# Two more landing places for the first weights, and a new order for every operation of a one-core attention and feed-forward kernel

## The chip, the cores and the metric

The kernel runs on one core of a Trainium2 chip. The core has a matrix engine (TensorE, PE in the profile), a vector engine (VectorE, DVE), a scalar engine (ScalarE, ACT), a general engine (GpSimd, POOL) and a queue engine (SyncE, SP) that here issues every DMA transfer. Each engine works through its own instructions in the order in which the program gives them, and waits on semaphores for the others. The metric is device time in microseconds.

## What is computed

Attention over four batches of eight heads with 768 positions of 64 values each: every position sees its neighbours nearer than 16 positions and, beside them, one maximum of the keys and one mean of the values for each of 24 blocks of 32 positions. Its output, 4 x 768 rows of 512, goes through a normalization and a feed-forward layer with a residual:

```python
scores_l = scale * np.matmul(q, k.transpose(0, 1, 3, 2))        # where |i - j| < 16
scores_s = scale * np.einsum('bhsd,bhnd->bhsn', q, k_sum) + np.log(block)
a = softmax(np.concatenate([scores_l_m, scores_s], axis=-1))
x = a @ np.concatenate([v, v_sum], axis=2)                      # heads side by side: 512
xn = (x - mu) / np.sqrt(var + 1e-06) * g_ln
out = x + np.maximum(xn @ w_ch1, 0.0) @ w_ch2                   # 512 -> 2048 -> 512
```

The two weights reach the kernel as eight bytes an element, so each is 8 MB in 16 tiles of 512 KB.

## The kernel before

**Tiles and stages.** The rows are cut into 24 tiles T of 128, taken in pairs g (12 pairs) by the feed-forward layer. The first batch's six tiles are done early, in 12 halves t, in float32 and straight from the inputs: `early_k` copies the window of the keys into a cleared buffer (POOL and ACT), `early_qk` multiplies (PE), `softmax` (DVE, then ACT), `early_transp` and `early_pv` (PE). The other three batches go through `heads` in split float16. `ln` normalizes a tile, `lnT` transposes it by DMA. `g1(s)` makes a 256-wide part of the middle values h of one pair (24 matrix instructions of 256 columns), `g2(s)` adds its part to the output (12 more, of 512 columns; "a" in the profile). 96 such parts make the feed-forward layer.

**Weights.** For each tile f of w1, `fetch_w(f, 1)` brings 512 KB into a buffer with the tag `raw`, of which there are four (RAW = 4), taken in turn; `merge_w` (one TENSOR_SCALAR and two SCALAR_TENSOR_TENSOR on DVE) makes 32-bit values m of it, after which the buffer is free; `gram` and, for each quarter of w1, `scale_w1` find a scale; `split_w` makes the two float16 halves that `g1` multiplies by. The same is done for w2, whose one scale (`scale_w2`) needs all 16 tiles. No `g2` can start before that.

**Middle values.** The values h lie in 14 buffers, taken in turn, each for two steps s: `y0` and `y1` first (YB = 2), then twelve buffers `x0` to `x11` that hold keys, queries and values of the early attention before.

**The order.** The program first records 2808 operations (an operation is one instruction, or a few of PE that stay together) with what each depends on. Then `Plan.issue` chooses the order in which they are given to the engines: `schedule` is a list scheduler with assumed durations and waits, which lets each engine take, of the operations that are ready, the one with the lowest rank. Before, the rank was worked out from the longest path to the end plus one stored number for each step (`ORDER`), improved in three rounds of a schedule forward and a schedule backward (`ROUNDS`), and then shifted by one stored number for each step and engine (`SHIFT`); a last schedule gave the order. Nothing of it exists on the chip but that order: an instruction there starts when its engine comes to it and what it depends on is done.

Of the kernel before, what the change touches and what calls it, by code (L numbers as in the profile page):

```python
# [19 lines left out]
U32 = mybir.dt.uint32  # L20
# [6 lines left out]
P = 128  # L27
# [16 lines left out]
ROUNDS = 3  # L44
# [17 lines left out]
    "rD2DqDep@g{w+NjZZ>8QypmT2yyg*W*&Alv&PatHNeiDt3tOdH_Kiay1!Yp{CvZ*8yC8neHYtX8Q@}Bf8dChtZr*`&;@_dh>3<+LnwafqmOH@g"
    "L*9>yF<TO1=0wi*Xe=5|mY|~*5$t`^Yzw*=4fn+tSbI%sJuhdGSqzvY<x3INzVJ&a5v+YS!G))p%R1^oS6=8RA3hz)X-"
    "gBe@0M=B#SHY3g)U+~mo}lNkXup^Jbg?2fz-DKOuT=RuA&!*KcW@%8}PE(X0%fCgjxJXwD?;y=V#Duq**jN%YpwGwAX&M^cFpmPwbliN=v=X8b"
    "_P82gAX{^8({yu&IEr&Ob<RyokQ3FN>O1p|$N`eC;)}$9TVFzFEJnW{E@DKiKS<$I+}2e}P%p5Om|q9^xMZ!w}ZIfOZD7V*$0i&EMJe(sttYU1"
    "(NAkF_J;Pr*JBF5}3h?^*EpOnTPKYyyAxp+--"
    "%JDiwZs3CEJ*|KPKMID#G^)UKv2{hXuW;Pd0+<Sn@N@?a4vu_C7LOu!9dlG%TOJ2_r@5S+Ej`T`AdmHeN0q7(j?4scDI(_gH`aVO?A1Ia@&}$h"
    "QcR~BLW6kbgrB~2W&)=bCxClYJS?*?Oc+w<#-3JWLqQ779fxnacIzRfCc-`ST0{*KirB<IQ{*ivhcf!!zB`|-"
    "VXEfTrL4WxYs{~z)B$u)1=aE)i(be2X%`(vJ&v?!e>aEMBhxi^qzKxye|0pn~XWZfPYy<r9bVCQe<d%evX5a}<DR?6K@`8`jUS_e>9t_ql=w~O"
    "mJ&m6GliPzjsRQ^HvS)--8>YSSnkW~ul2(mv$3M_W5ghKu>&C*z=9y-TIj{Mm6b^R<=*|HwLdpG=-"  # L70
    "<u7Fi>Q8R6kg`h%l>F{7MMG6hAVyOk6uQDMJ_peqLuHSH=EV!+w|e%=;k6Z9wpWh-uGnRsz1Ro-qqCIY#JWF9&Kc@zi9=&OTTt+q-"
    "W^KfIp+NJbdxGv>KoHK|dS7`=wZB31^;0kMDu&LF#etZ*~RT%Zc;)A@U=Bf4prnG5&(DucWRQ*3kF#XCZ#(LLYDa1%Do9=1m``5GMhj-"
    "3wkhY0?+?Rwr;shO0&E;V?^@jYrQ!I}vc#fjn2SCVani3;!#?!|KrFc)o{n)<iTjFPGlHD_c0v6J8t0Gn8K4$R2OJsTXSlnMa@Cp_6wJ3s3bW#"
    "sPkd-<59Tg`umYCy4Eh52c`yJmUV9brs~ioxGfRABRRxv)+?^+jtkxFPu8MvNoNc2j6n>zb5idWUU*#=6x^S2cHq-"
    "Sb%Ql^V|vMo$!UdpQ2TG^8?3HX43H4W`5Kf!|y8k9z|d7p=aKqPuz;g58Ri6XAy>y8DzGN`Es8)<#_T@`tBxrPJpL7_?QQ}d<dp-oD;;^325de"
    "&T_!F3(-PX@-9N_3z!vE<P}M+6Tl&XXYE|GNa|^a2YwB9{W#Z;^-"
    "<)WON}0!yAfU8#BV;wUpMm%;`=#%=lQ+Kx{mnqJC~%xtc{>2Iug5ro@t=(yMbjY{ho_XGFP_gG4%h>`h9KB<9)enaK@L+Mt`*Khj-PX>q@k;8("
    "-M*74wGL50cMP@GK?YE@*Q(-yNr${Q&pwub90$6@O-bGhQ8ncE-`i>FD|)Ga?eb1TX`7fK_Y1MS@e0SLrG6F2U2wUZ-"
    "!E@4vuDGB|nSiAEeZJiiv4nkV5&XxXEM`stZ-@RG{?D;B=jl4BYDca44vWY&eil{?=T!c7`nw)X3Ba&Tl8rsH2ie?x-X=I<uFY9c-"
    "F!~G|cdOjf5d1`$CE_HbBKJZ)1-RCLvA?_$k=P)nUwQ2btYuA3kOa{+#=3)uwI?@9bVEH|s)Xe{<&@I;vJBiLu@V*I-"  # L80
    "FHmbTGoUWi%!_&}iG2gy+`f_C&Tiu*6})aUhc4suG4y*fx;18mE1De2y>K4f72pBO$)g=-bU<j+z-&D+@8M-"
    "N#EPRgqPYhRV@=w|HqRP|e%BML3eT-1u{r3j1g{&32ffCfg3)7n_(#@%z=&G2$?Xhxfh6jzC%?<|{(N-"
    "5pFEwJ0lmoMBD__TTQ#^G9l_nK^&W>VmXrIkLChlJ_CcRl@Z=xiyP6s1OMhKpE;=y73pwWmnpi!~Y&x~oaDFAcIN^_>c&i^Xw-"
    "Jug$)^R4xiYUam@k?1*CFO@5_i>DJbeKAIE*I*qN{pz(=ncYqqbvsSUSAaFbf{iZ%goCSMU!b?+M^hPF*$l*iblH%)MqZ|L<XsC-"
    "ZU_XZ{Z!wza_"
)
SHIFT = (
    "c-n<q34B%6(SO-NLV_TRtP(&Pftm`aZ3=z}h@?tE5<w!Os9;1=MA?LovI%aVh*1{V6cA9$5*9(x3W8CQAZ;ytAR?6=0z%j!$?Jde{+BoJzPWk%"
    "{Vw;ubLY%{X6DSf_<X^?(qH}liGII-R+-"
    "=LtKcvFMELuMFWGbE8@P(jhmSpKz|A$rc3%x2J5w4ycAvq^dSmQ0fB4*)QQ>gi4PJgS=8iPR#u#&J8E}&g{$>DfNsQ0eAJ4Iz)8<^@o@?l$hC%"  # L90
    "D;3*loQoeLdHG3Mo;4j)@lDV)c3m&4&YT?rq{y*_;IABqBSA651Cx3`r&cE$R92jc_J&&S&ESr`5O_AZ}z9sW63>0uE0D=Q9;#Q@*49z3Ka!3S"
    ";(Jm2a8Qw@A&oeib?d1arkYE1BVY~{fHUyAoM@OGQACSJw(ku!dOwg<frjWu`BfSYqN2-"
    "hgl=Nm;iUcb)9I}^IwToj6XHpbc{2Y>hG`(nlSKIo{qM;yq9-"
    "!!cic;0)}hWS10T;TGh4Cu5hDfoK;=awqEIaTcS9tB%$2EM;|#Ixcv;o}b(>$0ArHRp)m|8$MObIA!CZx!GucCD{lF!rF*cOK<@_h=BVE7m|Vb"
    "g<u8ukGPCqbWz_DBEsR5x-BlWIc+t5Tk6_hP)>!|I2}0YUBQ^3vVW_ZCEE0J?!<GF?PVv-x~GY8~pu)_<lTT<1L8x`8Gv|j{Smp$%>CLq|-"
# [24 lines left out]
    "PWkXE`XQ6s@_w1@7ka%d;M;>9*hm$_l#G1N@T9RD!oy}tln4;8@WCP!TAc|S4D`w&Kk_Y{WkjA+sw^Vix6|5(-"  # L120
    "Gj|w5oyjGoCft7aV(;a{r*@ch2J`sQy$e*YslLZ)2HHo2yvs^k6PHJmb2a{C!E=&c%AH#I;aFU33MnbLa<$3HKLVEh%R&zLWE@34C@~-"
    "UgUP#FtYR+^^0iUqguF2<$Ww^fqB)G47+m*Q18rk6`>$&goBD2s!>Dj#VRn9|C_N>8&pd#=2<wW()At(j$h|r++M0esYP=eHGjyjNL1-"
    "*(1)sNdAU{r$xBtL9R^ddm-L!z#TvRFA@F^(&yrHH_EdQ0LLlQI_BCFu-^hlf6kdCY`fK|NocoJzzkx|kVW5p3-"
    "s<FzAmtJ9}gXT;P9mUKgBr@arGX5=L_A3>AxQ2GY@p758n?yI^3!Gq?X3KAECbj2TuHic7KMnuZn%C|DJgF3yhHqWBysuxnivSrkFDcSCq2j%~"
    "rofVl{Y3QvSBus{b(d46bzwuF!y!zI8f)-"
    "%@L@vB96Lt4zq)Th&Z`4Scfy!gk$1P~q!h$nhL#bc7tS3Qkh?A{A#=yL?seJw{31b@isM1KnM&+VBhbWM%SsfO5^g6x^#hXQk4I>&Url`K|!=z"
    "CvF)gm<5K^sc%S|NE*wI6%KnQ1Xe55i<Q<5^evxi?H`&9kdjGN6vR@$lYQi@U<Cyv?d?2&exN_81gQCy*7NmfpYu=8J%xprV`&sjJ?J=rwN~md"
    "n{%6n7l}zHG}-hcL(2l<o~~O{71F6ZgYC9N(bU^C*|zf<C~Nkw1<2LAbD^R;0Dmn@;%9<_`sRb1Y-"
# [37 lines left out]
class Plan:  # L166
# [174 lines left out]
    def schedule(self, rank, after, back):  # L341
# [16 lines left out]
        for _ in range(count):  # L358
# [27 lines left out]
            if e == "sync" and not back:  # L386
                t = max(t, flight[0])
# [855 lines left out]
```

## Time and profile before

| | us |
|---|---|
| time, median of 3 runs | 616.39 |
| lowest and highest | 614.54 and 616.79 |
| profiled execution | 614.86 |
| its span, first to last instruction | 613.0 |
| around the span | 1.9 |

A busy share on the page is that of the span. The 40 digits of a row on the page are slices of 15.3 us. A bracket at the end of a timeline row gives the idle time of the engine just before the instruction and what ended it. Every operation is recorded by one helper, so all rows show its line, L425, and are told apart by the names of the tiles. Ends of matrix instructions are modelled: neighbours overlap in the rows, and what one costs in a dense stream is the distance between starts.

### The profile page before, as it was taken

The numbers are of one execution on the slowest core, as the hardware profiler recorded it, in microseconds if no ns is written. First come the engines' busy times: TensorE is split into PE (matmuls) and PEld (weight loads), VectorE is DVE, ScalarE is ACT, GpSimd is POOL, SyncE is SP. The second block draws the span as 40 slices with busy tenths as digits, with TensorE's granted clock in tenths as the row PEclk, the third lists the DMA queues.
The fourth block names the chain that finished last, engine by engine and source line by source line (L and its number), as shares of the span: only waits on it lengthen the run. The fifth ranks groups of instructions, "written<-read, shape, count | busy, mean of one in ns | idle before, by whom it ended". The sixth has DMA issues, their size and how long they took to land.

```text
span 613.0 us, 14238 instructions
## 1 busy us (share of the span) xinstructions
PE 602.3 (98%) x5347; PEld 414.0 (68%) x5347; DVE 399.4 (65%) x1098; ACT 343.9 (56%) x914; POOL 151.9 (25%) x279
## 2 busy tenths in 40 slices
PE   6999999999999999999999999999999999999997
PEld 5557778885454685676767864666775676678756
DVE  5799999998568379767694487367486574412211
ACT  3689986578867458576864364366465644111100
POOL 7232312102324124321331033133142333100000
PEclk9999999999999999999999999999999999999999
DMA  8989897454677636867886045526466332300000
GB/s 302 281 251 329 236 298 234 115 145 127 178 208 197 167 100 167 214 138 197 200 176 171 14 127 136 130 77 178 120 154 162 89 94 53 62 10 1 17 18 35
DMA packets 116396, 90.56 MB, mean 148 GB/s; under 512 B 69613, under 2 KB 100717, under 8 KB 116326
## 3 DMA queue, kind: packets, MB, share of 16 engines
q1 hardware_dynamic: 116326, 89.65, 54.1%
q8 instruction: 42, 0.69, 0.5%
q14 instruction: 28, 0.23, 0.1%
HBM read 67.05 MB, written 6.29 MB: 120 GB/s over the span
## 4 chain that ended last, share of the span: by engine, by line
PE 76%; DVE 10%; DMA 6%; ACT 4%; issue 2%; SPq 1%; POOL 1%; ACTq 0%; POOLq 0%
PE h L425 33%; PE a L425 31%; PE s L425 3%; DVE m L425 2%; PE o L425 2%; DMA bst<-in_ks 2%; PE low L425 2%; DMA bst<-in_qa 2%; SPq L425 1%; PE warm L425 1%; DVE kmax L425 1%; DMA qs<-in_qt 1%; DMA bst<-in_vs 1%; DVE h_x L425 1%; ACT p L425 1%
## 5 line engine op out<-in xcount | busy, mean ns | idle before, releaser
L425 PE MATMUL h<-xt,w_u 128*128 128x256 f16 x2304 | 264.1, 273 | 0.0
L425 PEld LDWEIGHTS <-w_u 128*128 128x128 f16 x2304 | 224.1, 98 | 37.1 <-issue 0.9
L425 PE MATMUL a<-w,h_x 128*128 128x512 f16 (+1 forms) x960 | 211.5, 374 | 0.1
L425 PEld LDWEIGHTS <-h_x 128*128 128x128 f16 x1008 | 97.8, 98 | 98.7 <-issue 0.4
L425 ACT ACTIVATE h_x<-h 128x512 f16<-128x512 f32 x80 | 46.8, 591 | 96.7 <-PE h L425 96.4
L425 DVE SCALAR_TENSOR_TENSOR h_x<-h,h_x 128x512 f16<-128x512 f32 x80 | 54.5, 684 | 68.1 <-ACT h_x L425 68.0
L425 ACT ACTIVATE p<-p,mn,sv 128x120 f32<-128x120 f32 x144 | 68.2, 475 | 10.0 <-POOL mn L425 9.9
L425 POOL TENSOR_TENSOR p<-p,p 128x480 f16<-128x480 f32 x36 | 42.5, 1184 | 64.1 <-ACT p L425 59.8
L425 ACT ACTIVATE bst<-bst 128x384 f32<-128x384 f32 (+2 forms) x55 | 32.3, 588 | 33.0 <-DVE vsum L425 12.7
L425 POOL TENSOR_SCALAR mn<-mn,sv 128x4 f32<-128x4 f32 x36 | 17.7, 491 | 114.4 <-DVE mn L425 110.4
L425 PE MATMUL a<-w,h_y 128*128 128x512 f16 x192 | 43.9, 379 | 0.0
L425 DVE SCALAR_TENSOR_TENSOR m<-raw,m 128x512 uint32<-128x512 uint32 x64 | 42.9, 681 | 0.2
L425 DVE SCALAR_TENSOR_TENSOR kl<-ksg,sv,kh 128x640 f16<-128x640 f32 x36 | 33.3, 925 | 11.6 <-ACT kh L425 11.3
L425 DVE CUSTOM_DVE_ANT_0 p<-s,mask 128x120 f32<-128x120 f32 x144 | 33.2, 274 | 11.1 <-PE s L425 9.1
L425 POOL TENSOR_TENSOR x<-x,rc 128x256 f32<-128x256 f32 x36 | 25.2, 706 | 52.1 <-DVE x L425 50.0
L425 DVE SCALAR_TENSOR_TENSOR qhl<-qs,sv,qhl 64x512 f16<-64x512 f32 x36 | 28.1, 779 | 12.2 <-ACT qhl L425 11.3
L425 ACT ACTIVATE v<-vst,sv 128x512 f16<-128x512 f32 x36 | 24.4, 712 | 19.6 <-PE o L425 17.8
L425 DVE SCALAR_TENSOR_TENSOR x<-a,scales,x 128x512 f32<-128x512 f32 (+1 forms) x24 | 17.7, 736 | 26.7 <-PE a L425 26.6
L425 ACT ACTIVATE kh<-ksg,sv 128x640 f16<-128x640 f32 x36 | 29.5, 819 | 9.3 <-DMA ksg<-in_kt 6.9
L425 ACT ACTIVATE qhl<-qs,sv 128x512 f16<-128x512 f32 x36 | 25.7, 713 | 13.6 <-DMA qs<-in_qt 10.2
L425 PEld LDWEIGHTS <-h_y 128*128 128x128 f16 x192 | 18.6, 98 | 20.2
L425 DVE SCALAR_TENSOR_TENSOR v<-vst,sv,v 128x512 f16<-128x512 f32 x36 | 27.2, 772 | 2.0 <-ACT v L425 1.9
(118 smaller groups left out, 698.8 us busy)
## 6 DMA issues: line engine op xcount, KB each, us to landing
raw<-in_w SPq DMA_DIRECT2D x32, 512.0 KB
ksg<-in_kt SPq DMA_DIRECT2D x36, 368.0 KB
qs<-in_qt SPq DMA_DIRECT2D x72, 128.0 KB
out_x<-x SPq DMA_DIRECT2D x23, 256.0 KB
bst<-in_ks SPq DMA_DIRECT2D x20, 192.0 KB
bst<-in_qa SPq DMA_DIRECT2D x15, 256.0 KB
bst<-in_vs SPq DMA_DIRECT2D x20, 192.0 KB
vst<-in_va SPq DMA_DIRECT2D x36, 96.0 KB
```

The costliest lines, as they stand in the source:

```text
L425: getattr(getattr(nc, self.ops[i].engine), op)(*a, **k)
```

## The change

`fetch_w` puts the raw tiles f = 4 and f = 5 of w1 into the buffers `y0` and `y1`, which are as large, 4096 bytes in each partition; the first values h to use these buffers (those of s = 0 to 3) then also depend on `merge_w(4)` and `merge_w(5)`. The four `raw` buffers are left to the other 14 tiles of w1, and to w2 as before.

`ORDER` becomes a table of 2808 numbers, one for each operation, in the order in which they are recorded; `SHIFT` and the rounds are gone. Each number, times 16 ns, is a wanted time, and the rank is this wanted time. `schedule` holds every operation back until 600 ns (AHEAD) before its wanted time. No matrix instruction, vector instruction or transfer is added or removed.

```diff
-ROUNDS = 3
 ORDER = (
...
-SHIFT = (
...
-    FLIGHT = 8
+    FLIGHT, AHEAD = 8, 600
...
-    def schedule(self, rank, after, back):
+    def schedule(self, rank, after):
...
-                heapq.heappush(coming[self.ops[i].engine], (0.0 if back else 1000.0, i))
+                heapq.heappush(coming[self.ops[i].engine], (max(1000.0, rank[i] - self.AHEAD), i))
...
-                    heapq.heappush(coming[self.ops[j].engine], (ready[j], j))
+                    heapq.heappush(coming[self.ops[j].engine], (max(ready[j], rank[j] - self.AHEAD), j))
...
-        rank, best = [r + early[x.stage] for r, x in zip(rank, self.ops)], None
-        for _ in range(ROUNDS):
-            start, end = self.schedule(rank, after, False)
-            if best is None or max(end) < best[0]:
-                best = (max(end), start, end)
-            rank = [-x for x in self.schedule([-x for x in end], then, True)[1]]
-        rank = [r + shift[x.stage, self.ENGINES.index(x.engine)] for r, x in zip(best[1], self.ops)]
-        self.start, self.end = self.schedule(rank, after, False)
+        wanted = np.cumsum(np.frombuffer(zlib.decompress(base64.b85decode(ORDER)), "<i4"))
+        self.start, self.end = self.schedule(16.0 * wanted, [self.waits(x) for x in self.ops])
...
-        d = raw[f, i] = work("raw", f"raw{i}_{f}", [P, DM, 2], U32, RAW)
+        if i == 1 and f in (4, 5):
+            d = raw[f, i] = place(f"y{f - 4}", "raw", [P, DM, 2], U32)
+        else:
+            d = raw[f, i] = work("raw", f"raw{i}_{f}", [P, DM, 2], U32, RAW)
```

The new table can be unpacked and its numbers laid beside the operations of the kernel before. They are scattered, many are negative (first of all), and they are ranks rather than times of the chip. Those that the prediction speaks of:

```
operation (engine)                                   wanted, us
early_k(0), copies of the first key window (POOL)    -60.0 to -51.1
clear(): kx, second half (POOL)                       10.5
clear(): ends of the key rows (POOL)                  -41.0, -33.7, -26.0, -1.5, -0.2, 14.8, 14.8, 15.5
clear(): vst0 (POOL)                                  24.5
batch_k(0, 0), maximum of the keys (DVE)             -40.8
gain(), maximum over the broadcast gain (DVE)        -39.1
fetch_w(5, 1), fetch_w(4, 1), into y1 and y0 (SP)     14.7, 21.7
fetch_w of w2, the last three (SP)                    89, 92, 95
fetch_w of w1, all 16 (SP)                            at most 46.3
gram (PE), merge_w (DVE)   median of wanted less the start in the profile before: -14.6, -9.0
```

## Rows read from the trace of the kernel before

**Rows 1.** The page's line of busy times: engine, busy us (share of the span) x instructions.

```profile
PE 602.3 (98%) x5347; PEld 414.0 (68%) x5347; DVE 399.4 (65%) x1098; ACT 343.9 (56%) x914; POOL 151.9 (25%) x279
```

**Rows 2.** Busy time in four stretches that cover the span: from the start to the first h (44.8 us), from there to the first g2, from there to the end of the last matrix instruction, and the rest. Columns: stretch in us, its length, then busy us (x instructions) of PE, PEld (weight loads), DVE, ACT and POOL, granted TensorE clock, DMA share, GB/s.

```profile
0.00:45.00 45.00, 37.87 (x344) 24.52 (x345) 34.25 (x118) 28.48 (x95) 20.01 (x80) 0.96 0.89 277
45.00:134.50 89.50, 89.42 (x883) 71.83 (x882) 84.43 (x242) 69.50 (x203) 18.04 (x39) 1.00 0.79 234
134.50:609.70 475.20, 475.04 (x4124) 317.60 (x4121) 280.26 (x741) 245.96 (x618) 113.85 (x161) 1.00 0.47 120
609.70:613.00 3.30, 0.00 (x0) 0.00 (x0) 0.47 (x1) 0.00 (x0) 0.00 (x0) 1.00 0.12 40
```

**Rows 3.** The timeline of PE in the first 45 us, some of its rows: start, length, instructions; in brackets the idle time before and what ended it.

```profile
1.86 6.67 PE L425 MATMUL warm<-ident 128*128 128x128 f32 x36 [1.86 <-POOL ident masks.py:199]
...
11.49 0.67 PE L425 MATMUL s<-spare_x,spare_x 64*64 64x128 f32 x16 [1.65 <-POOL spare_x L425]
14.02 0.44 PE L425 MATMUL s<-ident 128*128 128x128 f32 x1 [1.86 <-DVE mn L425]
14.39 1.17 PE L425 MATMUL s<-spare_x,spare_x 64*64 64x128 f32 x16
15.49 1.11 PE L425 MATMUL pp<-ident,p 128*128 128x128 f32 x4
16.40 1.05 PE L425 MATMUL gram<-m 128*128 128x128 bf16 x8
...
20.76 0.44 PE L425 MATMUL pp<-ident,p 128*128 128x128 f32 x2 [0.44 <-DVE m L425]
...
21.24 0.67 PE L425 MATMUL s<-spare_x,spare_x 64*64 64x128 f32 x16
21.84 0.66 PE L425 MATMUL pp<-ident,p 128*128 128x128 f32 x4
...
35.15 0.65 PE L425 MATMUL s<-spare_x,spare_x 64*64 64x128 f32 x12 [0.67 <-ACT pT L425]
...
38.46 1.12 PE L425 MATMUL low<-m,diag 128*128 128x512 f32 x2 [0.31 <-ACT w_u L425]
...
44.32 0.64 PE L425 MATMUL gram<-m 128*128 128x128 bf16 x8
```

**Rows 4.** The end of the timeline: the last matrix instructions and the last vector instruction.

```profile
605.55 4.09 PE L425 MATMUL a<-w,h_x 128*128 128x256 f16 x36
...
609.69 0.48 DVE L425 SCALAR_TENSOR_TENSOR x<-a,scales,x 128x256 f32<-128x256 f32 x1 [3.45 <-PE a L425]
```

**Rows 5.** Two pieces of the chain of work that ended last: start, length in us, what ran, how many matrix instructions.

```profile
262.02 5.24 PE h L425 x48
267.27 1.29 PE a L425 x6
```

**Rows 6.** Busy time as in rows 2, in three short stretches.

```profile
10.00:12.50 2.50, 0.67 (x16) 0.42 (x16) 2.43 (x7) 0.60 (x2) 1.21 (x10) 1.00 1.07 383
12.50:15.00 2.50, 0.98 (x13) 0.79 (x17) 2.47 (x13) 2.44 (x11) 1.06 (x7) 0.78 1.09 381
15.00:17.50 2.50, 2.50 (x28) 1.98 (x20) 2.05 (x12) 1.64 (x7) 1.14 (x4) 0.54 1.09 386
```

**Rows 7.** Instructions on the buffers y0 and y1 as middle values, with their count, duration in ns (shortest, median, longest), and first and last start in us.

```profile
L425 PE MATMUL a<-w,h_y x192: 379/379/390, 134.5 to 600.1; 128*128 128x512 f16 x192
...
L425 ACT ACTIVATE h_y<-h x16: 571/597/621, 48.0 to 563.4; 128x512 f16<-128x512 f32 x16
```

**Rows 8.** Busy time as in rows 2 without PEld and POOL, of the instructions on h alone, from 40 us to the first g2.

```profile
40.00:134.50 94.50, 61.77 (x540) 14.29 (x21) 12.90 (x22) 1.00 0.79 231
```

**Rows 9.** The instructions on the raw tiles, w1 and w2 together, columns as in rows 7.

```profile
L425 DVE SCALAR_TENSOR_TENSOR m<-raw,m x64: 653/682/721, 6.1 to 116.4; 128x512 uint32<-128x512 uint32 x64
L425 SPq DMA_DIRECT2D raw<-in_w x32: 327/380/541, 1.5 to 105.4; - x32
L425 DVE TENSOR_SCALAR m<-raw x32: 396/419/776, 5.7 to 111.7; 128x512 uint32<-128x512 uint32 x32
```

**Rows 10.** The queue engine's waits in the first 60 us: what it waited for, us in total, times, longest.

```profile
SPq L425 <- DMA raw<-in_w: 4.8, 6, 1.3
SPq L425 <- DVE m L425: 4.8, 6, 1.7
```

**Rows 11.** The timeline of POOL from 8 to 12 us.

```profile
8.35 0.61 POOL L425 MEMSET spare_x<- 128x15 f32 x4
8.89 0.98 POOL L425 MEMSET vst<- 128x512 f32 x2
9.83 0.25 POOL L425 MEMSET spare_x<- 128x17 f32 x4
10.12 0.24 POOL L425 COPY spare_x<-spare_x 128x64 f32<-128x64 f32 x1
...
11.23 0.20 POOL L425 COPY spare_x<-kmax 128x24 f32<-128x24 f32 x1 [0.52 <-DVE scales L425]
```

**Rows 12.** The timeline of DVE, three rows between 6 and 11 us.

```profile
6.12 1.42 DVE L425 SCALAR_TENSOR_TENSOR m<-raw,m 128x512 uint32<-128x512 uint32 x2
9.62 0.69 DVE L425 TENSOR_REDUCE scales<-gain 128x1 f32<-128x512 f32 x1 [2.08 <-PE gain L425]
10.22 0.94 DVE L425 TENSOR_REDUCE kmax<-spare_x 128x24 f32<-128x768 f32 x1
```

More of the change, by code (lines that the diff above doesn't have):

```diff
@@ L62 @@
[L62 to L83, printed above, removed]
@@ new lines @@
+    "=ZnJk~VE+(E{#m>cHTE8$uWq#!;{0mTGimIKTKyfgLa5X;-"
+    "Y;99(JUU4BbHCAy|EHck_Z2!rpSqolsN+R?%w`uezc$Sa*fp!yUOhM=Ep!*)WRE|_*WplY+p4s6C@ZB9^{?9?h6^dCDgNE3;%Fo=SybbVIIj{d"
+    "gV-GseSxG{$Y08)J9S5EHSuDQOUH2_;<+5}y?TfJcX}@w(0h>=4?KLb^S@|=3kEAI7&<B}Y!fOmA=-"
+    "SzpukAroHv6FNV)@a~mY*lR6jn}%@3MS<9BTgB0%TgEHv{&`bYRbN3gC>_n+>$?@O|8~SYP?|+o_f>mwk-#@21+|-"
+    "i7uhcy?qzrc*1|{hMdDXrpU+Cs4ds9Lu39HkZsgFXO<?%9xGRi{Mu#-"
+    "Taoml%>9IC(*Y_x&{A&@*>JV@ts7w6n!UX@1>oe_F7~NfyN;8yvD!3+JXN+-"
+    "$rX6j{|oD^UuTgNAj=qUZA)We8qKh19nG@WDh2?dB68_+Msx^`|-"
@@ L155 @@
+    "ioocd1=i~Jt_SAl0svAw7`TX_}branlwc(?%TsTgP%@{PnmDE?^xd}p}*2d`U-<)OwXrqW)~n+!#EQg5Q!v{(Ieauz-"
+    "4|38tQ`Et6`rMKF^f0Rz3tN-"
+    "V`=D(@WPPKUPU;izlNVxsKNat00?L@6NuHL$bm9J;qstn5kCMZXp+4h`#=lU3&6WJYSEpy(JZ2m;FpMO*?NAcJSc=kljc;tECHNRc&Micce8)1"
+    "I0@_xO1o%d8OP4DfLJn&6=Z22GMCrU!k)qgFd8~O{SnSO)5uOeOT)V&U%p#F0MT>r;aUR&|SOk|Od@-"
+    "V~pqwcD5;HK%F1N;NfUdQ;B>E?UtKOfy(`)}a?0TcFZc>"
 )
@@ L351, in schedule @@
         coming, waiting = ({e: [] for e in self.ENGINES} for _ in range(2))
-        ring, warm, columns, tick = 0.0 if back else self.FIRST, False, 0.0, 0.0
+        ring, warm, columns, tick = self.FIRST, False, 0.0, 0.0
         port, half = 0.0, 0
@@ L375, in schedule @@
                 half = self.ops[i].half
-            if e == "tensor" and not back:
+            if e == "tensor":
                 while t >= tick + self.TICK:
@@ L385, in schedule @@
                 columns += (t + busy - at) * per
-            if e == "sync" and not back:
+            if e == "sync":
                 t = max(t, flight[0])
@@ L389, in schedule @@
             if e == "sync":
-                ring = max(ring, t if back else t + self.BEGIN) + moving
-                if back:
-                    free[e] = max(free[e], ring)
-                end[i] = ring + (self.BEGIN if back else 0)
+                ring = end[i] = max(ring, t + self.BEGIN) + moving
                 flight = flight[1:] + [ring + self.ops[i].tail]
@@ L398, in schedule @@
                 if not left[j]:
-                    heapq.heappush(coming[self.ops[j].engine], (ready[j], j))
+                    heapq.heappush(coming[self.ops[j].engine], (max(ready[j], rank[j] - self.AHEAD), j))
         return start, end
     def issue(self, nc):
-        after = [self.waits(x) for x in self.ops]
-        then = [[] for _ in after]
-        for i, x in enumerate(after):
-            for j, wait in x:
-                then[j].append((i, wait))
-        rank = [0.0] * len(after)
-        for i in reversed(range(len(after))):
-            x = self.ops[i]
-            rank[i] = min((rank[j] for j, _ in then[i]), default=0.0) - x.busy - x.moving - (self.WAIT[x.engine] or x.tail)
-        table = lambda x: 16.0 * np.frombuffer(zlib.decompress(base64.b85decode(x)), "<i4")
-        early, shift = table(ORDER), table(SHIFT).reshape(-1, len(self.ENGINES))
-        rank, best = [r + early[x.stage] for r, x in zip(rank, self.ops)], None
-        for _ in range(ROUNDS):
-            start, end = self.schedule(rank, after, False)
-            if best is None or max(end) < best[0]:
-                best = (max(end), start, end)
-            rank = [-x for x in self.schedule([-x for x in end], then, True)[1]]
-        rank = [r + shift[x.stage, self.ENGINES.index(x.engine)] for r, x in zip(best[1], self.ops)]
-        self.start, self.end = self.schedule(rank, after, False)
+        wanted = np.cumsum(np.frombuffer(zlib.decompress(base64.b85decode(ORDER)), "<i4"))
+        self.start, self.end = self.schedule(16.0 * wanted, [self.waits(x) for x in self.ops])
         self.time = max(self.end)
-        for _, i in sorted(zip(self.start, range(len(after)))):
+        for _, i in sorted(zip(self.start, range(len(self.ops)))):
             for op, a, k in self.ops[i].calls:
```

162 lines of the change are left out of this document (86 added, 76 removed).

## The prediction

> **What bounds the kernel now.** The page's line of busy times comes first: the matrix engine is busy 98% of the span, the vector engine 65% [rows 1]. Then the span by stretches [rows 2], where the reader is to look for idle time of PE. From the first h at 45 us to the last matrix instruction at 609.7 us PE is busy 89.42 + 475.04 of 564.7 us: it idles 0.24 us in all. The idle time lies at the two ends. The first 45 us have 45 - 37.87 = 7.13 us of it, of which 1.86 us pass before the first matrix instruction of all [rows 3]; that leaves 5.27 us. The last 3.3 us hold one vector instruction of 0.48 us and the last output transfer [rows 4], which no order can do without.
>
> Is a busy PE a full one? In the chain of waits 48 instructions of h take 5.24 us, 109 ns each, and 6 of a take 1.29 us, 215 ns each [rows 5]; 256 and 512 columns at the upper clock level, 2.4 GHz, are 106.7 and 213.3 ns. The dense part is full to within 2%. The granted clock is 1.00 in it and 0.96 in the first 45 us [rows 2]. So PE's own work sets the time; a new order can win only what is lost before 45 us, and can lose as much as it likes.
>
> The timeline of PE names that loss [rows 3]: 1.65 us until POOL has put together the first key window, 1.86 us until the vector engine has finished the first softmax rows, then 0.44, 0.67 and 0.31 us, and 0.34 us in pieces that are not shown. The clock adds to it. After the first two gaps the granted clock is 0.78 and then 0.54 in the stretches from 12.5 and 15 us, which is 1.2 GHz for nearly all of the second [rows 6]. What that costs is read from equal work: 16 instructions of s take 1.17 us there and 0.67 us later, four of pp 1.11 and 0.66, eight of gram 1.05 and 0.64 [rows 3]: 0.50 + 0.45 + 0.41 = 1.36 us. All that can be won is 5.27 + 1.36 = 6.6 us.
>
> **Does an early gain reach the end?** PE has no idle time to absorb it, but it must have work. Until the first g2 at 134.5 us [rows 7] it lives on h of the first three pairs, 3 x 8 x 24 = 576 instructions, of which 540 are done by then [rows 8]. What is left is 36 x 109 ns = 3.9 us. If PE comes 3.9 us earlier and g2 does not, PE idles. And g2 hangs on the vector engine, which is busy 84.43 of the 89.5 us before it [rows 2] and merges the last weights at 116.4 us [rows 9]. So up to 3.9 us pass through freely; beyond that the merges must move too.
>
> **The change part by part.** Nothing is added or removed on any engine, so its terms are all waits.
>
> *Two more landing places.* A raw tile costs the vector engine 419 + 2 x 682 ns = 1.78 us [rows 9], after which its buffer is free. In the first 60 us the queue engine waits six times, 4.8 us in all, for such a merge before it may issue, and as long for landings of raw tiles [rows 10]; every key, value and query that follows in SP's queue waits with it. Two of the 16 tiles no longer take a raw buffer, so about two of the six waits go, some 2 x 0.8 = 1.6 us of SP's time, between nothing and 4.8. This is no time of PE. What it allows is that two merges, 3.6 us of vector work, move from the stretch where that engine is 94% busy into the first 45 us, where it idles 45 - 34.25 = 10.75 us [rows 2]. The new table asks for this: merges are wanted 9 us, grams 14.6 us earlier than they ran, and the last three fetches of w2 at 89 to 95, where the last one ran at 105.4 [rows 9]. The new wait is that of the first h in y0 and y1, written from 48.0 us on [rows 7]. Behind it stand ACT's queue and, with two buffers for h in PSUM, PE itself. The two fetches are wanted at 15 and 22, more than 20 us ahead, and the merge takes 1.78: I cost the wait at nothing. If the cover were gone it would cost what the merge is late, one for one. DMA, 0.89 busy before 45 us [rows 2], leaves little room for more than a tile or two ahead of time.
>
> *The first gap, 1.65 us.* POOL clears for 0.61 + 0.98 + 0.25 us right before its first copy at 10.12 [rows 11]. The table puts half of the 0.98 (vst0), the second half of kx and some of the ends behind the copies: about 1.2 us. But the copy for which PE waits is that of the key maxima at 11.23, and it waits for the vector engine, which takes the maximum at 10.22 behind the reduction of the gain at 9.62, for which it idled 2.08 us [rows 11, 12]. The table turns these two around: 10.22 - 9.62 = 0.6 us. The bounds are nothing (if the keys land no earlier than the gain, the order stays) and 1.65. I take 0.6.
>
> *The second gap, 1.86 us.* It is the same chain one step on, with two more maxima and four softmax rows on the vector engine; DMA is at 1.07 to 1.09 of its share there [rows 6], so the keys themselves are late. Work that could fill it is the gram of the first raw tile, merged by 7.54 [rows 12], half of the 0.64 us that eight instructions take [rows 3]. Bounds 0 and 1.86; I take 0.5, near that filler.
>
> *The three later gaps and the pieces*, 0.44 + 0.67 + 0.31 + 0.34 = 1.76 us, are waits of a few tenths for a merge, a copy, a weight, which other work can hide once merges and grams are wanted earlier. Bounds 0 and 1.76; I take half, 0.9.
>
> *The clock*, 1.36 us, comes back if the first two gaps no longer let it fall, and they remain for 3.5 - 1.1 = 2.4 us by my terms. Bounds 0 and 1.36; I take half, 0.7.
>
> The Trainium skill says of this ("TensorE: Matmul & The Clock Gate", section "HAM oscillation — how this bites in real kernels") that idle gaps between matrix instructions make the gate slow the engine, so that the next work starts cold. The trace agrees: 0.54 of the clock after the two gaps [rows 6]. By the rule alone, gaps that stay would cost the whole 1.36 us again, and the gain would be 0.7 us smaller.
>
> *New losses.* The old order idles 0.24 us after 45 us; the nearest estimate for a new order made by the same kind of planner is as much again, 0.2 us. From below it is nothing; from above it has no bound but the rivals'.
>
> Sum: 0.6 + 0.5 + 0.9 + 0.7 - 0.2 = 2.5 us, within the 3.9 us that pass through. The profiled execution would go from 614.86 to 612.4 us. It was 1.5 us under the median of 616.39, so as a median I say 613.9 us, 0.4% less. About 0.5%, 3.1 us or a median of 613.3, is what a measurement of this kernel can tell from no change.
>
> **The rivals.** *Small gain* is the case above, 612.5 to 615.4 us: 0.50.
>
> *Nearly all of it*: both first gaps close, the clock stays up, and the earlier merges bring g2 forward: 4 to 6.6 us, 609.8 to 612.4 us. For it speaks that one wanted time per operation can put any filler into any gap; against it that DMA is at its limit there [rows 6] and that the clock needs both gaps gone. 0.27.
>
> *The gain is given back*: the extra buffers do nothing because the transfers are hidden anyway, or PE runs ahead and then waits for the first g2, since the vector engine is 94% busy before it [rows 2]. The time stays at 615.4 to 617.5 us. 0.12.
>
> *Slower*: the scale of w2 needs the merges of all 16 tiles, and a new order that puts other vector work ahead of a single one of them delays every g2. The reserve is 3.9 us; beyond it each us costs one. It decides from a delay of about 3.9 + 2.5 + 3.1 = 9.5 us on; at 10 us the median is 616.39 + 10 - 6.4 = 620.0. Against it: the table wants merges and fetches earlier. 0.09.
>
> *PE is not full after all.* Matrix instructions in the dense part take 109 and 215 ns for 106.7 and 213.3 [rows 5]; over 2304 and 1152 of them that is 5.3 + 2.0 = 7.3 us, which would give 609.1 if an order could win it. No row shows one that runs faster. 0.02. The Trainium skill warns here ("Trainium Kernel Development and Optimization", section "Best Practices") that matmul busy time says little of the distance to the limit and that the busy share of weight loads is to be read, 68% here [rows 1]; by that a third of the span would be open. The distances between starts say otherwise [rows 5].
>
> **How the numbers follow.** Faster by over 0.5% are "nearly all", "not full" and the lower end of the small gain: 0.27 + 0.02 + 0.05 = 0.34. Slower by over 0.5% is the slower case and a little: 0.10. The rest, 0.56, lies within. The range of 8 in 10 reaches from nearly everything won, 609.8, to a gain given back with some loss, 617.6.
>
> **What would show it.** Right: idle time of PE before 45 us falls from 7.1 to about 5 us, the first s starts near 10.9 us, the stretch from 12.5 to 17.5 us has a higher clock, the first h and the first g2 come some 2 us earlier, and the idle time between 45 us and the last matrix instruction stays under 1 us. Wrong: a wait of PE for merged weights or for h between 100 and 140 us, a later first g2, ACT waiting for a merge before its first h in y0, or gaps at the start as long as now.

## The result: slower by 0.7%, and where the profile puts it

The changed kernel takes 621.19 us in the median (616.13 to 623.6) where the kernel before takes 616.5: a ratio of 1.0074, 95% interval 1.0055 to 1.0093. It is slower, by about 4.6 us, and outside the range that was given. The profiled execution is one of its fastest, 617.11 us with a span of 615.3; most are some 4 us longer, so its trace shows only half of the loss, and the traces of the experiments have to show the rest.

Busy time in the first three of the four stretches, as in [rows 2] (the first h comes at 43.7 us, the first g2 at 135.4):

```profile
0.00:45.00 45.00, 37.81 (x357) 24.29 (x358) 35.59 (x126) 29.49 (x100) 17.61 (x80) 0.92 0.92 279
45.00:134.50 89.50, 87.26 (x851) 68.91 (x849) 82.43 (x229) 66.52 (x193) 15.37 (x36) 1.00 0.80 225
134.50:612.00 477.50, 477.33 (x4144) 319.50 (x4141) 283.49 (x744) 248.99 (x622) 111.50 (x163) 1.00 0.48 121
```

Read against [rows 2]: PE idles 45 - 37.81 = 7.19 us before 45 us, where it idled 7.13. It idles 2.24 us from 45 to 134.5 us, where it idled 0.08. Behind that, 0.17 for 0.16. The span grew by 2.3 us, and 2.16 of them lie in the second stretch.

PE's timeline before 45 us, the two gaps that answer to those of [rows 3]:

```profile
11.14 0.67 PE L403 MATMUL s<-spare_x,spare_x 64*64 64x128 f32 x16 [1.90 <-POOL spare_x L403]
14.04 0.45 PE L403 MATMUL s<-ident 128*128 128x128 f32 x1 [2.23 <-DVE scales L403]
```

And from 45 to 136 us, its five longest waits, each for another engine:

```profile
52.80 1.13 PE L403 MATMUL low<-m,diag 128*128 128x512 f32 x2 [0.33 <-ACT w_u L403]
54.88 0.55 PE L403 MATMUL pp<-ident,p 128*128 128x128 f32 x3 [0.62 <-ACT p L403]
72.87 5.40 PE L403 MATMUL h<-xt,w_u 128*128 128x256 f16 x48 [0.24 <-DVE h_y L403]
119.47 1.47 PE L403 MATMUL h<-xt,w_u 128*128 128x256 f16 x12 [0.42 <-DVE vm L403]
127.35 1.49 PE L403 MATMUL h<-xt,w_u 128*128 128x256 f16 x12 [0.34 <-DVE h_x L403]
```

Both first gaps stayed and are longer than before, 1.90 and 2.23 us for 1.65 and 1.86. The five later waits are short and for five different tiles. Between the first two gaps and behind them the granted clock is lower than in [rows 6]; columns as there:

```profile
12.50:15.00 2.50, 0.96 (x13) 0.76 (x17) 1.73 (x14) 1.84 (x11) 0.85 (x5) 0.50 1.09 384
15.00:17.50 2.50, 2.50 (x18) 1.61 (x11) 2.23 (x13) 2.21 (x11) 1.00 (x4) 0.50 1.09 385
17.50:20.00 2.50, 2.50 (x30) 1.37 (x29) 2.48 (x12) 1.60 (x7) 0.64 (x4) 0.78 1.09 385
```

The new order isn't needed for that: in the traces of mid225 and old262 (below), whose order is the old one up to 225 us, the granted clock is 0.50 from 12.5 to 17.5 us as well.

The vector engine's timeline shows why the first gap stayed, and one copy of POOL tells when the next keys landed:

```profile
4.20 0.95 DVE L403 TENSOR_REDUCE kmax<-spare_x 128x24 f32<-128x768 f32 x1 [4.20 <-DMA spare_x<-in_ks]
7.36 1.15 DVE L403 TENSOR_SCALAR m<-raw 128x512 uint32<-128x512 uint32 x1 [2.21 <-DMA raw<-in_w]
8.54 1.42 DVE L403 SCALAR_TENSOR_TENSOR m<-raw,m 128x512 uint32<-128x512 uint32 x2
9.88 2.67 DVE L403 TENSOR_REDUCE kmax<-spare_x 128x24 f32<-128x768 f32 x3
12.47 0.68 DVE L403 TENSOR_REDUCE scales<-gain 128x1 f32<-128x512 f32 x1
13.06 0.28 DVE L403 CUSTOM_DVE_ANT_0 p<-s,spare_x 128x128 f32<-128x128 f32 x1
```
```profile
9.06 0.27 POOL L403 COPY spare_x<-spare_x 128x64 f32<-128x64 f32 x1 [0.84 <-DMA spare_x<-in_ks]
```

In the kernel before, two rows that [rows 12] leaves out:

```profile
5.66 0.43 DVE L425 TENSOR_SCALAR m<-raw 128x512 uint32<-128x512 uint32 x1 [0.60 <-DMA raw<-in_w]
...
12.50 0.29 DVE L425 CUSTOM_DVE_ANT_0 p<-s,spare_x 128x128 f32<-128x128 f32 x1
```

The key maxima do go ahead of the gain, as the prediction said. The merge of the first raw tile stands ahead of both in either kernel, but in the kernel before it waits 0.60 us for its tile and is done by 7.54. Now DVE waits 2.21 us, the first step takes 1.15 us for 0.43, and the merge is done by 9.96. By POOL's copy the keys had landed by 9.06, so the merge holds the next maximum for up to 0.8 us. That maximum starts at 9.88 us for 10.22, and the first s at 11.14 for 11.49: 0.35 us are won there. They are lost one step on. Two more maxima and the gain now stand on DVE ahead of the first softmax row, which starts at 13.06 us for 12.50, and the second gap ends at 14.04 us for 14.02.

The two new landing places, as the trace has them: the fetches into y0 and y1, the first step of their merges, and ACT's first values in them.

```profile
L403 SPq DMA_DIRECT2D raw_y<-in_w x2: 368/610/853, 10.6 to 16.3; - x2
L403 DVE TENSOR_SCALAR m<-raw_y x2: 419/420/420, 18.0 to 26.2; 128x512 uint32<-128x512 uint32 x2
```
```profile
L403 ACT ACTIVATE h_y<-h x4: 591/606/626, 49.1 to 72.0; 128x512 f16<-128x512 f32 x4
```

The merges are done by 28.5 us, 20 us before ACT needs the buffers; no engine waits for them. In the first 60 us SP waits four times for a merge where it waited six times [rows 10], but 5.3 us in all for 4.8; its waits for landings of raw tiles fall from 4.8 us to 1.3.

### The profile page after: what moved, and what is told of

It reads as the page before. It is cut to its first block, busy times and chain, and to the rows that moved or that the text cites. A ratio compares the mean times of both kernels' runs of the same rounds, so it can differ in the third digit from the quotient of the medians.

```text
span 615.3 us, 14225 instructions
## 1 busy us (share of the span) xinstructions
PE 602.4 (98%) x5347; PEld 412.7 (67%) x5347; DVE 402.0 (65%) x1098; ACT 345.0 (56%) x914; POOL 144.5 (23%) x279
## 4 chain that ended last, share of the span: by engine, by line
PE 79%; DVE 10%; DMA 5%; ACT 3%; SPq 1%; issue 1%; POOL 0%; ACTq 0%; DVEq 0%
PE a L403 37%; PE h L403 32%; DVE m L403 4%; PE s L403 3%; PE o L403 2%; DMA raw<-in_w 2%; DMA bst<-in_ks 2%; PE v L403 1%; DVE h_x L403 1%; DVE kmax L403 1%; PE last L403 1%; SPq L403 1%; ACT p L403 1%; DMA vst<-in_vb 1%; PE low L403 1%
## 5 line engine op out<-in xcount | busy, mean ns | idle before, releaser
L403 DVE SCALAR_TENSOR_TENSOR m<-raw,m 128x512 uint32<-128x512 uint32 x60 | 40.1, 684 | 0.3
L403 POOL TENSOR_SCALAR mn<-mn,sv 128x4 f32<-128x4 f32 x36 | 16.4, 455 | 91.1 <-DVE mn L403 84.6
L403 DVE SCALAR_TENSOR_TENSOR v<-vst,sv,v 128x512 f16<-128x512 f32 x36 | 29.5, 825 | 2.5 <-ACT v L403 2.5
L403 ACT ACTIVATE x<-xn,rs 128x512 f16<-128x512 f32 x24 | 17.1, 714 | 23.7 <-DVE rc L403 10.4
```

What stands on the lines that cost most here:

```text
L403: getattr(getattr(nc, self.ops[i].engine), op)(*a, **k)
```

## Experiments: the buffers or the order

All ratios below are to the kernel before, run beside on the same chip, with 95% intervals.

**ord_only** takes the buffers out and keeps the new order (its `ORDER` holds the planned starts of the changed kernel, with AHEAD = 0, so that the order stays):

```
-        if i == 1 and f in (4, 5):
-            d = raw[f, i] = place(f"y{f - 4}", "raw", [P, DM, 2], U32)
-        else:
-            d = raw[f, i] = work("raw", f"raw{i}_{f}", [P, DM, 2], U32, RAW)
+        d = raw[f, i] = work("raw", f"raw{i}_{f}", [P, DM, 2], U32, RAW)
```

> The new order with the buffer part undone: all 16 raw tiles of w1 in the four raw buffers, the order on every engine as in the changed kernel (but two neighbouring vector instructions). Theory 'order' (the loss of 4.7 us lies in the new order, between 45 and 134.5 us): 620 to 622 us, the matrix engine idle 2 us or more in that stretch. Rival 'buffers' (the new wait of y0 and y1, or the other turn of the raw buffers, costs it): 616 to 617.5 us. Rival 'start' (the clock, which falls lower at the start): 620 to 622 us as well.

Measured 620.83 us, ratio 1.0082 (1.0053 to 1.0110), the changed kernel's being 1.0074: the whole loss, with PE idle for 3.76 us between 45 and 134.5 us. In the traces the order of the two kernels is the same on ACT, POOL and SP, and on DVE but for one instruction. So the order makes the loss; no share of the buffers is to be seen within these intervals.

**buf_only** has the buffers and the old order as wanted times, **new_start** the buffers, the new order to 46 us and the old one behind, **new_rest** the old order to 46 us and the new one behind, without the buffers. In all three the scheduler may still move what does not fit:

```
-FLIGHT, AHEAD = 8, 600
+FLIGHT, AHEAD = 8, 0
-ORDER = (the new wanted times)
+ORDER = (old and new planned starts, joined as said)
```

> The order before with the buffer part alone: raw tiles 4 and 5 in y0 and y1; only what the other turn of the raw buffers forces is moved (the later raw fetches wait for other merges than before, and what hangs on them). Theory 'order': no loss from y0 and y1 themselves, but where the old order does not fit the other turn a few us may be lost; 616 to 620 us, and no wait of the matrix or scalar engine for a merge of y0 or y1. Rival 'buffers': 620 us or more with a visible wait behind y0 or y1.

> Old buffers and the old order for everything planned before 45 us, the new order for the rest. Theory 'order after 45 us': 619 to 622 us, with the matrix engine idle 2 us or more between 45 and 134.5 us. Rival 'start': 616 to 617.5 us.

> New buffers and the new order for everything planned before 45 us, the old order for the rest. Theory 'order after 45 us': 616 to 618 us. Rival 'start' (the granted clock is 0.50 from 12.5 to 17.5 us and 0.78 after, instead of 0.78 and 0.54): 620 to 622 us.

Measured: buf_only 621.56 (ratio 1.0076 to 1.0109), new_rest 621.73 (1.0062 to 1.0102) and new_start 620.47 (1.0047 to 1.0098). Two of them say less than they seem to: the scheduler moved other operations as well, by the traces 42 of the 240 instructions of DVE between 46 and 136 us both in buf_only and in new_start, though the order there was to be the old one. They show that two more orders lose 4 to 6 us as well. new_rest came out as meant: in its trace DVE, ACT, POOL and SP have the old order before 46 us and the changed kernel's behind it, but for an instruction or two. It loses 5.4 us, so the whole loss can arise behind 46 us, as its theory said; PE's idle time between 45 and 134.5 us is 1.51 us, less than the 2 expected.

## Experiments: which stretch

From here on the order is written down operation by operation, with nothing left to the scheduler and the four raw buffers of the kernel before:

```
-        self.start, self.end = self.schedule(16.0 * wanted, ...)
+        self.start = wanted        # the place in the list seq
 new46 :  seq = [new order, planned before 46 us]  + [all others in the old order]
 new136:  seq = [new order, planned before 136 us] + [all others in the old order]
 old136:  seq = [old order, planned before 136 us] + [all others in the new order]
```

> Four raw buffers as before. The new order up to 45 us, then exactly the old one, instruction by instruction. Theory 'each stretch pays its own' (the old order fits the landing times of its transfers everywhere, any other fits them less, and each reordered stretch costs for itself): 617 to 618.5 us, the loss seen before 45 us only. Rival 'the start upsets all that follows': 620 to 622 us, with new idle time of the matrix engine after 200 us although the order there is the old one. Rival 'late stretch' (the loss is made after 136 us): 616 to 617 us.

> Four raw buffers. The new order up to 135 us, then exactly the old one. 'Each stretch pays its own': 618 to 620 us, idle time between 45 and 135 us as in the changed kernel (2 us or more), none after. 'The start upsets all': 620 to 622 us. 'Late stretch': 616 to 617 us.

> Four raw buffers. The old order up to 135 us, then the new one. 'Each stretch pays its own': 618 to 620 us, idle time of 2 to 4 us between 200 and 330 us, none between 45 and 135 us. 'The start upsets all': 616 to 617 us. 'Late stretch': 620 to 622 us.

Measured: new46 615.72, ratio 0.9993 (0.9976 to 1.0009); new136 617.91, 1.0032 (1.0017 to 1.0047); old136 619.16, 1.0046 (1.0030 to 1.0063). So the new start neither wins nor loses within its interval. The stretch from 46 to 136 us costs 617.91 - 615.72 = 2.2 us, and all behind it 619.16 - 616.22 = 2.9. Together with the start, -0.5, that is 4.6 us: the whole loss. The traces bear the expected places out for old136 (PE idles 0.11 us between 45 and 135 us and 3.55 between 200 and 330) and only in part for new136 (1.57 us where 2 or more were expected, and 2.36 between 135 and 330, where none was). They are of one execution each: new46's idles 1.37 us between 45 and 135 us, where its order is the old one from 46 us on.

**shake10** and **shake3** ask whether the new table is a bad one: the old order, with each planned start moved at random by up to 1.0 or 0.3 us.

> Four raw buffers. The old order shaken: every operation's planned start is moved by a random amount of up to 1 us either way, and the operations are put in that order as far as their dependencies allow; nothing of the new table. Theory 'the old order is fitted, any other of the same kind costs': 619 to 623 us, as much as the new table. Rival 'the new table is bad in itself': 616 to 617.5 us.

> The old order with each planned start moved at random by up to 0.3 us either way (shake10 had up to 1 us, 690.9). Theory 'most orders near the old one lose, in proportion to what is moved': 620 to 640. Rival 'only large moves cost': within 1.5 us of the kernel before, 616.5.

Measured 690.88 us (1.1184 to 1.1241) and 622.24 us (1.0059 to 1.0115). What was expected of shake10 fell, by far. A random move of up to 0.3 us, less than one DVE instruction on h, costs as much as the whole change; each shake is one draw. Nor does the loss go with the number of instructions moved: to turn the old order into shake3's, 69 of DVE, 14 of ACT and 7 of SP have to be moved in the traces (instructions of the same names and shapes taken in turn), into shake10's 203, 122 and 75, into the changed kernel's 359, 220 and 150. So the new table isn't bad in itself: it moves more than either shake and loses no more than the smaller one, 4.6 us for 5.1. PE's longest waits in shake10, us in total, times, longest:

```profile
PE h L346 <- DVE h_x L346: 18.6, 12, 7.0
```

**sp45** is the old order with SP's queue alone in the new one from 46 to 136 us.

> The old order, with the order of SP's queue alone taken from the new one between 45 and 135 us (80 fetches and transposes, of which 31 would have to be moved to turn one order into the other); PE, DVE, ACT and POOL keep the old order. That stretch with all engines new cost 2.2 us (new136 617.9 against new46 615.7). Theory 'the order of the fetches makes the raw tiles and the batches of keys land late': +1.5 to +2.5, 617.8 to 618.8 us. Rival 'it is the order in which DVE and ACT work (109 of 218 and 72 of 155 moved)': within 0.6 us of the kernel before, 616.3.

Measured 626.06, ratio 1.0171 (1.0147 to 1.0195): 9.5 us, four times what the stretch costs with all engines new. PE waits for h_x there, five times:

```profile
PE h L345 <- DVE h_x L345: 6.4, 5, 1.9
```

Neither theory holds. The fetch order isn't bad in itself: with the other engines in the new order too the stretch costs 2.2 us. It is bad beside queues that belong to another order; DVE's or ACT's new order alone was not tried.

## Experiments: the loss between 45 and 135 us

In the changed kernel's trace the w2 merges have one outlier, the longest in DVE's row on raw tiles; then the timelines of DVE and POOL around it:

```profile
L403 DVE TENSOR_SCALAR m<-raw x30: 395/419/2104, 7.4 to 113.1; 128x512 uint32<-128x512 uint32 x30
```
```profile
112.73 2.44 DVE L403 TENSOR_SCALAR m<-raw 128x512 uint32<-128x512 uint32 x2
```
```profile
112.87 2.02 POOL L403 MEMSET p<- 128x2048 f16 x1 [1.93 <-DVE m L403]
```

The second of the two TENSOR_SCALAR takes 2.10 us for the usual 0.42, as long as the memset beside it runs. The kernel before has the same memset, with other instructions beside it:

```profile
111.71 0.41 DVE L425 TENSOR_SCALAR m<-raw 128x512 uint32<-128x512 uint32 x1
112.04 1.28 DVE L425 SCALAR_TENSOR_TENSOR m<-raw,m 128x512 uint32<-128x512 uint32 x2
113.24 0.54 DVE L425 TENSOR_REDUCE kmax<-bst 128x12 f32<-128x384 f32 x1
```
```profile
112.08 1.81 POOL L425 MEMSET p<- 128x2048 f16 x1
```

SCALAR_TENSOR_TENSOR and TENSOR_REDUCE keep their usual length there. The stall is in all four traces that have this stretch in the new order on every engine (2.10 us in the changed kernel, new136 and new_rest, 1.87 in ord_only); in the traces with the old order there no such step of w2 takes over 0.8 us. A shorter one is in the DVE rows of the start, shown above: the first TENSOR_SCALAR, 1.15 us at 7.36, beside memsets of POOL from 7.53 to 8.23 us. **ts_move** is the changed kernel with that one instruction three places later:

```
 DVE:  TENSOR_SCALAR m (merge 15)
-      TENSOR_SCALAR m (merge 14)
       TENSOR_REDUCE kmax;  h_x;  SCALAR_TENSOR_TENSOR m (merge 15)
+      TENSOR_SCALAR m (merge 14)
       SCALAR_TENSOR_TENSOR m (merge 14)
```

> The changed kernel with one DVE instruction moved: the first step of merge 14 of w2 (TENSOR_SCALAR m from raw) goes behind the key maximum, one half of h and one step of merge 15, three places later, so that it no longer runs beside POOL's memset of p. In the changed kernel's trace it takes 2.10 us at 113.07, beside a memset of 2.02 us from 112.87, where 30 of the 32 such instructions take 0.4. Theory 'that one stall costs the stretch from 45 to 135 us most of its loss': DVE's 1.7 us come back, PE's waits for vm and h_x from 117 to 128 us (0.76 us there, 1.85 in ord_only) go, the time falls by 0.8 to 1.8 us, to 619.4 to 620.4. Rival 'the stretch loses by many small waits, or what is won is given back later': within 0.5 us of the changed kernel, 621.2. Rival 'another DVE instruction is stalled in its place': the same, with a long instruction beside the memset.

Measured 620.48, ratio 1.0046 (1.0022 to 1.0070), that is 1.7 us less than the changed kernel by the ratios and 0.7 by the medians, and the two intervals overlap. From the trace, DVE's timeline, and the stretch from 45 to 135 us:

```profile
112.61 0.42 DVE L347 TENSOR_SCALAR m<-raw 128x512 uint32<-128x512 uint32 x1
113.60 0.55 DVE L347 TENSOR_REDUCE kmax<-bst 128x12 f32<-128x384 f32 x1 [0.57 <-DMA bst<-in_ks]
...
115.27 0.42 DVE L347 TENSOR_SCALAR m<-raw 128x512 uint32<-128x512 uint32 x1
```
```profile
45.00:135.00 90.00, 89.61 (x872) 71.07 (x870) 84.07 (x236) 69.56 (x202) 15.36 (x36) 1.00 0.80 230
```

The long instruction is gone, and PE idles 0.39 us in this stretch, for 2.24. That the stall came from running beside the memset is shown. What its removal is worth in time isn't: in the trace of ts_q, below, which has the same move and no such step over 0.43 us, PE idles 1.68 us in this stretch, with a wait of 0.54 us for vm at 122.16 again.

## Experiments: the loss behind 136 us

In six of the seven traces with the new order behind 136 us (old136, pull_ln, ts_move, ts_q, ord_only, new_rest) PE waits at the same two places. The seventh is the changed kernel's own: with the same order it idles 0.11 us between 200 and 330 us. And old262, below, waits there in its trace, an execution of 619.80 us, though its median is 616.61. So these waits seem to come in some executions of an order and not in others, though no kernel has two traces to show it. Three of them, timeline of PE from 200 to 330 us:

```profile
266.33 1.04 PE L346 MATMUL a<-w,h_x 128*128 128x512 f16 x4 [0.35 <-DVE h_x L346]
293.39 2.78 PE L346 MATMUL h<-xt,w_u 128*128 128x256 f16 x24 [2.09 <-DMA xt<-x]
```
```profile
270.38 1.04 PE L364 MATMUL a<-w,h_x 128*128 128x512 f16 x4 [1.71 <-DVE h_x L364]
296.50 2.78 PE L364 MATMUL h<-xt,w_u 128*128 128x256 f16 x24 [1.15 <-DMA xt<-x]
```
```profile
268.45 1.04 PE L346 MATMUL a<-w,h_x 128*128 128x512 f16 x4 [1.28 <-DVE h_x L346]
293.94 2.78 PE L346 MATMUL h<-xt,w_u 128*128 128x256 f16 x24 [0.52 <-DVE h_x L346]
```

(old136, ord_only, old262.) The way back from old136's 293.39, first on DVE, then on ACT:

```profile
288.67 0.75 DVE L346 SCALAR_TENSOR_TENSOR qhl<-qs,sv,qhl 64x512 f16<-64x512 f32 x1 [1.96 <-ACT qhl L346]
289.45 0.75 DVE L346 SCALAR_TENSOR_TENSOR x<-xn,rs,x 128x512 f16<-128x512 f32 x1
...
292.79 0.68 DVE L346 SCALAR_TENSOR_TENSOR h_x<-h,h_x 128x512 f16<-128x512 f32 x1
```
```profile
280.05 0.63 ACT L346 ACTIVATE bst<-bst 128x512 f32<-128x512 f32 x1 [2.89 <-DMA bst<-in_qa]
...
282.96 0.83 ACT L346 ACTIVATE kh<-ksg,sv 128x640 f16<-128x640 f32 x1 [1.58 <-DMA ksg<-in_kt]
284.78 0.72 ACT L346 ACTIVATE v<-vst,sv 128x512 f16<-128x512 f32 x1 [0.99 <-DMA vst<-vsum]
...
286.57 0.63 ACT L346 ACTIVATE bst<-bst 128x512 f32<-128x512 f32 x1 [0.58 <-DMA bst<-in_qa]
...
287.92 0.72 ACT L346 ACTIVATE qhl<-qs,sv 128x512 f16<-128x512 f32 x1 [0.62 <-DMA qs<-in_qt]
...
289.16 0.57 ACT L346 ACTIVATE h_x<-h 128x512 f16<-128x512 f32 x1
```

The profile names xt. By the order of the code the same h also needs the PSUM buffer that DVE's h_x frees at 293.47, so the two come at about the same time. In this execution both hang on one instruction: the x from which xt is transposed (289.45) and, three microseconds of ready work later, h_x (292.79, though ACT had written its half by 289.73) stand on DVE behind qhl at 288.67, and qhl stands on ACT behind five waits for landings, 6.7 us between 277 and 288. No instruction here takes longer than usual: each engine does its list in order, and one late landing holds all that is listed behind it.

**pull_ln** (old136 with five operations of layer norm 9 taken ahead of a key maximum) and **ts_q** (ts_move with one fetch of bst taken ahead of four puts of vsum on SP) each move such a list:

> The kernel of old136 (old order to 135 us, then the new one; 619.2 us, 2.9 over the kernel before), with five operations of layer norm 9 and its transpose xt taken ahead of the key scales kmax of batch (3, 2) in the list: on DVE, ACT and SP xt's makers then no longer stand behind the landing of bst that kmax waits for. In old136's trace PE waits 2.1 us for that xt at 250 us, of 3.1 us that it idles between 200 and 300 us. Theory 'one engine's queue put xt's makers behind a landing': the wait is gone, PE's idle time between 200 and 300 us falls to about 1.0, the time to 617.1 +- 0.6. Rival 'the key chain itself is what is late, and what is let ahead makes it later still': the same time as old136, 619.2 +- 0.6, with PE waiting for kl or h_x instead. Rival 'it is no single wait, PE stands at another place in each execution': 618 to 620.

> ts_move with one SP instruction moved besides: the fetch of bst for batch_q (3, 1) goes ahead of the four puts of vsum into vst (3.15 us of SP's queue), as in the old order, where it is issued 4.7 us earlier. In old136 each later fetch of that batch, ACT's reading of it and what stands behind ACT and DVE came late with it, to PE's wait of 2.1 us at 293.39. Theory 'that fetch makes the late loss': 1.5 to 2.5 us below ts_move, 617 to 618.5. Rival 'the chain is late for other reasons as well': within 0.6 us of ts_move.

pull_ln: 619.31, ratio 1.0058 (1.0037 to 1.0079), no better than old136. Its premise was misread: old136's wait at 250 us is of 0.19 us, and the 2.09 are those at 293, so it doesn't test those. ts_q: 621.18, 1.0065 (1.0039 to 1.0091), no better than ts_move; the theory that this fetch makes the late loss falls.

Five more splices, made like those above, look for the place: **mid136** (new order from 136 to 225 us alone), **mid225** (225 to 262), **old262** (262 to the end), **mid262** (136 to 262) and **old225** (225 to the end).

> The old order, with the new one from 136 to 225 us alone (106 of 396 instructions of that stretch would have to be moved), both splices exact, raw tiles in the four raw buffers. old136 has the new order from here on and costs 2.9 us, mid225 (225 to 262 us alone) -0.7, old262 (from 262 us) 0.0. Theory 'the late loss is made in this stretch': +2 to +3.5, 618.5 to 620. Rival 'each stretch alone is harmless, the loss appears where one late stretch meets the next': within 0.8 us of the kernel before, 616.5.

> The old order, with the new one from 225 to 262 us alone (52 of 219 instructions of that stretch would have to be moved to turn one into the other), both splices exact, raw tiles in the four raw buffers. Theory 'the late loss is made where xt comes late at 250 us': +1.5 to +2.5, 617.8 to 618.8 us. Rival 'the late loss gathers over the whole of the late part, no stretch of its own': +0.2 to +0.8, 616.5 to 617.1. Rival 'a splice costs by itself': more than +3, 619.3 or above.

> The old order to 262 us, then exactly the new one, raw tiles in the four raw buffers. Theory 'the late loss is made before 262 us': within 0.6 us of the kernel before, 616.3. Rival 'it gathers over the whole late part': +1.5 to +2.5, 617.8 to 618.8. With mid225 and old136 (+2.9) the parts should add up.

> The old order to 225 us, then exactly the new one to the end, raw tiles in the four raw buffers: mid225 and old262 in one. Theory 'the loss appears where the stretch from 225 to 262 us in the new order meets the new order behind it': +2.3 to +3.5, 618.8 to 620. Rival 'the stretch from 136 to 225 us is needed for it': within 0.8 us of the kernel before, 616.5. The sum of the two single runs would be -0.7 to 0.

> The new order from 136 to 262 us alone, the old one before and behind: mid136 and mid225 in one. Theory 'the seam at 262 us makes the loss': within 0.8 us of the kernel before, 616.5. Rival 'the two early stretches together make it, and what stands behind only shows it': +2.3 to +3.5, 618.8 to 620. If neither this nor old225 loses, it takes the whole of the late order.

| new order in | us | ratio (95%) |
|---|---|---|
| 136 to 225 | 616.87 | 0.9995 (0.9977 to 1.0014) |
| 225 to 262 | 615.88 | 0.9989 (0.9970 to 1.0008) |
| 262 to the end | 616.61 | 1.0006 (0.9988 to 1.0025) |
| 136 to 262 | 616.52 | 0.9996 (0.9981 to 1.0012) |
| 225 to the end | 616.89 | 1.0007 (0.9989 to 1.0025) |
| 136 to the end (old136) | 619.16 | 1.0046 (1.0030 to 1.0063) |

No stretch behind 136 us loses anything by itself in the median, nor do two neighbours; the intervals leave room for 0.5 to 1.5 us. The 2.9 us appear only where the new order runs from before 225 us to beyond 262. Which instructions make them was not found, nor what decides whether a trace has the waits. Nor does the sum of waits for landings tell: between 200 and 330 us DVE, ACT and POOL wait 20.0 us for transfers in the kernel before, 30.0 in old136, and 32.8 in mid136, which loses nothing. This half stays open.

## Why the prediction was wrong, step by step

- **What bounds the kernel** held. PE is busy 98% in both, and nearly all of the difference in the profiled spans, 2.2 of 2.3 us, is idle time of PE.
- **The new wait of the buffers at nothing** held: fetches at 10.6 and 16.3 us, merges from 18.0, no wait, and ord_only loses as much without them. Two of SP's six waits for merges went, as counted, though the four that are left take 5.3 us for 4.8.
- **The start, 0.6 + 0.5 + 0.9 + 0.7 us of gain**, failed. new46 measures -0.5 us (-1.5 to 0.6), where these terms say -2.7. The first term named the right pair, gain and key maxima, and 0.35 of its 0.6 us came; it left out the merge ahead of both, which waits 2.21 us for its tile in place of 0.60. The second term was lost to the same exchange, which puts two maxima and the gain ahead of the first softmax row. The clock term was read from one execution, and 0.50 in place of 0.78 and 0.54 is found with the old start too (mid225, old262). That the DMA share was 1.07 to 1.09 there was in [rows 6]; the terms took what the table wants for what it would get.
- **New losses at 0.2 us** is the step that failed most: they are 2.2 us from 46 to 136 us and 2.9 behind. The estimate, "as much again" as the old order's 0.24 us, took the old order for one of many equal ones. shake3 shows that a neighbour need not be one: up to 0.3 us away, it loses 5.1 us. The 0.24 us were also those of one execution, 1.5 us under the median; new46's trace, with the old order behind 46 us, idles 2.0 us between 46 and 330. For the first stretch [rows 2] could have warned: DVE 94% busy, PE never idle. Behind 134.5 us DVE is busy 280.26 of 475.2 us, and no row warns of the 2.9; their cause stays open.
- **The rival "slower"** had the wrong mechanism. It wanted one delay of 9.5 us at the merges of w2. The last merge step starts at 120.8 us for 116.4 [rows 9], 4.4 us later and so past the reserve of 3.9, but the first g2 comes only 0.9 us later, at 135.4 for 134.5 [rows 7]. What cost time were waits of 0.2 to 2 us at many places: three of the four signs listed under "wrong" came true, a wait for h between 100 and 140 us, a later first g2, and gaps at the start as long as before. That the median lies near the 620.0 which this rival gives for a delay of 10 us is chance.

## What to carry to other kernels

Where one engine is full and four others feed it in listed order, a list that runs without waits can be worth several microseconds that no table of wanted times shows; give a new list a loss term, and measure what random shakes of the old one cost (5 us for moves of up to 0.3 us here, 75 for up to 1 us). Compare queues as a set: half of a new order (sp45) can be worse than all of it. Look for single instructions far above their usual length before blaming the order as such. And don't read a loss of a few microseconds from one trace: the changed kernel's shows half of its loss, and old262's shows waits that its median doesn't.

## What the runs showed of the hardware

A TENSOR_SCALAR of 128x512 uint32 on DVE took 2.10 us for 0.42 beside a memset of 2.02 us on POOL, while two SCALAR_TENSOR_TENSOR (1.28 us together) and a TENSOR_REDUCE (0.54) kept their length beside the same memset in the kernel before. The Trainium skill says so ("SBUF — State Buffer", section "Who interferes with whom"): a one-source vector instruction in a two-port mode and a GpSimd instruction take the shared port pair from each other for a whole instruction, while one with two SBUF inputs does not mind a GpSimd instruction that only writes. These traces agree in both halves; that TENSOR_SCALAR runs in such a mode no row shows by itself.
